# In the first three token pairs one expert's first layer goes by seven products instead of two, and the keys' copies and transposes of later attention groups are queued sooner

## The chip, the core and the metric

The kernel runs on one core of a Trainium2 chip. A core has five engines [...]: TensorE (PE, matrix products; its weight loads are listed as PEld), VectorE (DVE, element-wise work), ScalarE (ACT, exponentials, relu, copies), GpSimd (POOL, here mostly issuing casting loads) and SyncE (SP, issuing loads, stores and transposing transfers). [...] The metric is the device time of one execution in microseconds (us); smaller is better.

## What is computed

Causal attention, where some heads see everything and the others only four sink keys and a window of 64, followed by a mixture of four dense experts, each weighted by a normalised probability per token. Cut to what matters:

```python
# B, H, S, D = 4, 8, 768, 64;  N, DM, E, F = 3072, 512, 4, 1024
scores = q @ k.T / sqrt(D)             # masked: causal, or causal & (sink | window of 64)
a = softmax(scores)                    # per head; 3 heads "retrieval", 5 "streaming"
x = (a @ v).reshape(B * S, H * D)      # 3072 tokens x 512
p = domain_probs / domain_probs.sum(-1)
out = 0
for e in range(4):
    h = maximum(x @ w1[e], 0)          # first layer, 512 -> 1024
    out += p[:, e:e+1] * (h @ w2[e])   # second layer, 1024 -> 512
```

The probabilities are positive, so the kernel scales the inputs of an expert by p before its first layer: relu(p x w1) = p relu(x w1).

## The kernel before

The 3072 tokens are 24 tiles of 128. Attention is done in eight groups of 384 tokens (three tiles; group = batch element b and half c). The experts' work starts while attention is still going on: tiles 0 to 3 go expert by expert in the plain way, and then ten *pairs* of tiles (4 and 5, 6 and 7, ... 22 and 23) follow. Attention for groups 2 to 7 is recorded in small steps between the steps of the pairs; a plan says at which point of the pairs each group is to begin and to end:

```python
UNIT = FTP * DMP * mm_ns(CH) + 3 * FTP * mm_ns(DM)
ONE = E * (FTP * DMP * mm_ns(P) + FTP * mm_ns(DM))
PAIR = 2 * FTP * DMP * mm_ns(PC) + 2 * 7 * HT * KH * mm_ns(P) + 7 * KT * mm_ns(HN)

def att_ns(a):                         # length of a group's attention, for the plan
    ns = 4000.0 if a % NCH == 0 else 6100.0
    ns += NSH * (600.0 if a == 1 else 400.0)
    return ns + (600.0 + HP * 3 * 400.0 if a < NCH else 0.0)
...
begin = E * UNIT + 0.6 * ONE
for a, n in zip(range(2, G), (0.72, 1.65, 3.1, 4.3, 5.95, 7.38)):
    plan[a] = (begin, first_pair + n * PAIR)
    begin = plan[a][1]
```

A pair's first layer gives, per expert, four blocks of relu values in hA. Experts 0 and 1 do it plainly (32 matmuls of 256 columns and four relu evictions on ScalarE). Experts 3 and 2 (EW) do it by Strassen's seven products in Winograd's form (7 x 8 = 56 matmuls of 128 columns), which needs sums of inputs and of results on VectorE:

```python
def plain_layer1(e):                   # yields after each of 4 steps
    xs = scaled(e)
    for f0 in range(0, FTP, 2):
        ps = bank()
        for f in range(2):
            for ct in range(DMP):
                nc.tensor.matmul(out=ps[:, f * PC : (f + 1) * PC],
                    lhsT=w1sb[:, e * DMP + ct, (f0 + f) * P : (f0 + f + 1) * P], rhs=xs[:, ct, :], ...)
        nc.scalar.activation(out=blocks[...], in_=ps..., func=AF.Relu)
        yield 2 * DMP * mm_ns(PC), LSHARE

def scaled_sums(e):                    # three sums of inputs, VectorE
    nc.vector.tensor_tensor(out=x_sum(0), in0=x_part(e, 1, 0), in1=x_part(e, 1, 1), op=ALU.add)
    minus(x_sum(1), x_sum(0), x_part(e, 0, 0))
    minus(x_part(e, 1, 0), x_part(e, 0, 0), x_part(e, 1, 0))

def winograd_layer1(e, x, y):          # yields after each of 7 products of 8 matmuls
    def keep(n, ps): nc.scalar.copy(out=kept[n], in_=ps)
    def add(n, ps, b):                 # block b = relu(product + kept one), VectorE
        nc.vector.tensor_tensor(out=block(b), in0=ps..., in1=kept[n]..., op=ALU.add)
        nc.vector.tensor_scalar(out=block(b), in0=block(b), scalar1=0.0, scalar2=None, op0=ALU.max)
    product(x, w1_part(e, 0, 0), x_part(e, 0, 0), True);  keep(0, x);  yield ns, LSHARE
    z = bank()
    product(z, w1_part(e, 1, 0), x_part(e, 0, 1), True);  add(0, z, 0);  yield ns, LSHARE
    product(x, t(1), x_sum(1), False);  keep(1, x);  yield ns, LSHARE
    product(y, t(0), x_sum(0), True);  keep(2, y)
    minus(x_part(e, 0, 1), x_part(e, 0, 1), x_sum(1));  yield ns, LSHARE
    product(x, w1_part(e, 0, 1), x_part(e, 1, 0), False);  add(2, x, 3);  yield ns, LSHARE
    product(y, w1_part(e, 1, 1), x_part(e, 0, 1), False);  add(1, y, 2);  yield ns, LSHARE
    product(x, t(2), x_part(e, 1, 1), False)
    nc.scalar.activation(out=block(1), in_=x..., func=AF.Relu);  yield ns, LSHARE

a, b = (winograd_layer1(e, *y) for e, y in zip(EW, (banks, banks[::-1])))
n01 = itertools.chain(plain_layer1(0), plain_layer1(1))
early_on = dense(nt0)                  # the first three pairs
for steps, op in (
    ((a, a, n01), lambda: scale_inputs(nt0, EW[1]) if early_on else None),
    ((a, a, n01), lambda: load_probs(nxt) if nxt and not early_on else None),
    ((a, a, n01), lambda: scale_inputs(nt0, 1) if early_on else None),
    ((n01,), lambda: scaled_sums(EW[1])),
    ((a, b, n01), lambda: first_sum(0)),
    ((b, b, n01), lambda: load_probs(nxt) if nxt and early_on else None),
    ((b, b, n01), lambda: last_weight_sum(E - 1) if nt0 == pair0 else None),
    ((b, n01, b), lambda: first_sum(EW[0])),
):
    for x in steps: yield next(x)
    op()
first_sum(1); first_sum(EW[1])
```

The second layer of all four experts together follows, also by seven products, of 16 matmuls of 256 columns each (112 in all), in every pair; this change leaves it alone. Its VectorE work (differences of hA, additions of results, the scaling of the next pair's inputs) is recorded between its products. The sums of expert 2's first-layer weights (t1sb, four VectorE operations of 128x1024) are made while tiles 0 to 3 are worked on.

A group of attention in the later batches runs as follows; kT is one buffer that the transposing transfers of the next group overwrite:

```python
if by_dma:
    keys_to_rows(b, c)                 # kT -> kR, VectorE
    yield 500.0                        # counts as time in the plan
...
for n, h in enumerate(order):          # order = (0, 2, 6, 1, 3, 5, 7, 4)
    ...
    yield from both(scores(h), v_steps)
    ...
    if n == 1 and by_dma:
        keys_to_windows(b, c)          # kT -> kS, VectorE
        sink_rows(b, c)
    if n == 2 and more and g > 1:
        transpose_k(*more)             # the next group's keys -> kT
        load_q(*more)
    ...
if more:
    ...
    transpose_q(*more)
```

Of the kernel before, what the change touches and what calls it, by code (L numbers as in the profile page):

```python
# [18 lines left out]
def kernel(  # L19
# [34 lines left out]
    P = 128  # L54
    B, H, S, D = q.shape
    E, DM, F = moe_w1.shape
    CH = 3 * P
# [222 lines left out]
    def keys_to_windows(b, c):  # L280

        x = windows(kSf)
        for r, n0, hp0, n in ((1, 0, 0, 2), (1, 3, 2, 2), (0, 2, 2, 1)):
            r = half(r)
            src = kT[r, hp0 : hp0 + n, P - WO + NS :]
            step = src.ap[1][0]
            src = bass.AP(
                src.tensor, src.offset, [src.ap[0], [step, n], [WQ, WT], [1, P - NS]]
            )
            dst = x[r, :, n0 : n0 + n, :].rearrange("p t n x -> p n t x")  # L290
            nc.vector.tensor_copy(out=dst[:, :, :, NS:P], in_=src)  # L291
            if c == 0:
                src = kT[r, hp0 : hp0 + n, P : P + NS]
                src = src.rearrange("p n (t x) -> p n t x", t=1)
                nc.vector.tensor_copy(
                    out=dst[:, :, :, 0:NS], in_=src.to_broadcast([D, n, WT, NS])
                )
        if b * NCH + c + 1 < G:
            nc.vector.tensor_copy(out=kT[:, :, P - WO : P], in_=kT[:, :, CH + P - WO :])
# [231 lines left out]
    def mm_ns(cols):  # L531
        return cols / 2.4 + 2.5

    def attention(b, c):
# [282 lines left out]
        if first:  # L817
            yield from transposes(0)
            yield from scores(0)
            sink_row(1)  # L820
            sink_row(3)
            nc.scalar.copy(out=bS[:, 2, :], in_=bS[:, 1, :])
            yield from transposes(1)
            yield from scores(2)
            sink_row(4)
            sink_row(5)
            sink_row(7)
            yield from both(scores(1), values(0))
            yield from transposes(2)
            yield from both(scores(3), values(2))  # L830
            x_transposes(0)
            yield from scores(4)
            yield from transposes(3)
            yield from values(1)
            yield from both(scores(5), values(3))
            yield from both(scores(6), values(4))
            yield from both(scores(7), values(6))
            yield from values(5)
            x_transposes(6)
            yield from values(7)  # L840
            tick(LAG)
            small_things()
        else:
            order = (0, 2, 6, 1, 3, 5, 7, 4) if by_dma else (0, 2, 1, 3, 6, 5, 7, 4)
            more = divmod(g + 1, NCH) if g + 1 < G else None
            if not by_dma:
                sink_rows(b, c)

            def behind_values(h):
                if more and not RETR[h]:  # L850
                    load_v(*more, [h])
            if by_dma:
                keys_to_rows(b, c)
                yield 500.0
            else:
                yield from transposes(0)
                yield from transposes(1)

            waiting = []
            for n, h in enumerate(order):  # L860
                v_steps, done = iter(()), None
                ahead = sum(len(score_tiles(x)) for x in (*waiting, h))
                if len(waiting) > 1 or (waiting and ahead > 6):
                    done = waiting.pop(0)
                    v_steps = values(done)
                yield from both(scores(h), v_steps)
                if done is not None:
                    behind_values(done)
                waiting.append(h)
                if n == 1 and by_dma:  # L870
                    keys_to_windows(b, c)
                    sink_rows(b, c)
                if n == 2 and more and g > 1:
                    transpose_k(*more)

                    load_q(*more)
                if not by_dma and n in (1, 3):
                    yield from transposes({1: 3, 3: 2}[n])
            if more:
                if g == 1:  # L880
                    load_probs(pair0)
                    transpose_k(*more)
                transpose_q(*more)
            for h in waiting:
                yield from values(h)
                behind_values(h)
# [180 lines left out]
    def scale_inputs(nt0, e):  # L1067

        if xs_of[0] is None:
            xs_of[0] = moe.tile([P, E * DMP * PC], FP16, name="xs", tag="xs", bufs=1)  # L1070
        xs = scaled(e)
        for g, c0, t0, n in pieces(nt0):
            require(g)
            xin = xT[g][:, :, c0 : c0 + n * P].rearrange("p c (t x) -> p c t x", t=n)
            o = xs[:, :, t0 * P : (t0 + n) * P].rearrange("p c (t x) -> p c t x", t=n)
            pb = pB_of[nt0][:, t0 : t0 + n, e, :]
            pb = pb.rearrange("p t (c x) -> p c t x", c=1)
            nc.vector.tensor_tensor(  # L1078
                out=o, in0=xin, in1=pb.to_broadcast([P, DMP, n, P]), op=ALU.mult
            )  # L1080
# [25 lines left out]

    def dense(nt0):

        return nt0 < pair0 + 3 * PT

    def pair_steps(nt0, nxt):

# [89 lines left out]

        a, b = (winograd_layer1(e, *y) for e, y in zip(EW, (banks, banks[::-1])))
        n01 = itertools.chain(plain_layer1(0), plain_layer1(1))
        early_on = dense(nt0)
        for steps, op in (
            ((a, a, n01), lambda: scale_inputs(nt0, EW[1]) if early_on else None),  # L1210
            ((a, a, n01), lambda: load_probs(nxt) if nxt and not early_on else None),
            ((a, a, n01), lambda: scale_inputs(nt0, 1) if early_on else None),
            ((n01,), lambda: scaled_sums(EW[1])),
            ((a, b, n01), lambda: first_sum(0)),
            ((b, b, n01), lambda: load_probs(nxt) if nxt and early_on else None),
            ((b, b, n01), lambda: last_weight_sum(E - 1) if nt0 == pair0 else None),
            ((b, n01, b), lambda: first_sum(EW[0])),
        ):
            for x in steps:
                yield next(x)  # L1220
            op()
        first_sum(1)
        first_sum(EW[1])

        o = moe.tile([P, PT, DM], FP32, name="o", bufs=1)
        s = moe.tile([P, 4 * HN], FP32, name="s", tag="sums", bufs=1)
# [80 lines left out]
        add(1, y, 0, 1)  # L1307
        if nxt:
            scale_inputs(nxt, EW[1] if ahead else EW[0])
        store(0)  # L1310
        if last:
            store(1, 1)
# [13 lines left out]
    def moe_steps():  # L1326
        for e in range(E):
            if e == 1:
                turn_probs()
            sums = first_weight_sums(EW[1])[:3] if e == E - 1 else []  # L1330
            steps = plain_steps(0, 3, e, lambda: xT[0], (e % 2) * FTP * CH)
            for n, step in enumerate(steps):
                yield step
                if n > FTP and n % 2 and sums:
                    sums.pop(0)()
            for op in sums:
                op()
            weight_sums(e)
        sums = first_weight_sums(EW[0])
        for e in range(E):  # L1340
            n0 = (e % 2) * FTP * P
            for n, step in enumerate(plain_steps(3, 1, e, lambda: xT[1][:, :, 0:P], n0)):
                yield step
                if n == FTP - 1:
                    sums[e]()
                    if e == EW[1]:
                        first_weight_sums(e)[3]()
            if e + 1 < E:
                last_weight_sum(e)
                (  # L1350
                    lambda: scale_inputs(pairs[0], 0),
                    lambda: scale_inputs(pairs[0], EW[0]),
                    lambda: scaled_sums(EW[0]),
                )[e]()
        for n, nt0 in enumerate(pairs):
            yield from pair_steps(nt0, pairs[n + 1] if n + 1 < len(pairs) else None)
# [19 lines left out]

    UNIT = FTP * DMP * mm_ns(CH) + 3 * FTP * mm_ns(DM)
    ONE = E * (FTP * DMP * mm_ns(P) + FTP * mm_ns(DM))
    PAIR = 2 * FTP * DMP * mm_ns(PC) + 2 * 7 * HT * KH * mm_ns(P) + 7 * KT * mm_ns(HN)

    def att_ns(a):
        ns = 4000.0 if a % NCH == 0 else 6100.0
        ns += NSH * (600.0 if a == 1 else 400.0)
        return ns + (600.0 + HP * 3 * 400.0 if a < NCH else 0.0)

# [1 line left out]

    plan = {1: (1.15 * UNIT, 3.5 * UNIT)}
    begin = E * UNIT + 0.6 * ONE
    for a, n in zip(range(2, G), (0.72, 1.65, 3.1, 4.3, 5.95, 7.38)):  # L1390
        plan[a] = (begin, first_pair + n * PAIR)
        begin = plan[a][1]
    loads(2)
    state = {"a": 1, "steps": None, "done": 0.0}
# [76 lines left out]
```

## Time and profile before

| | before |
|---|---|
| device time, median of 3 | 393.79 us (393.74 to 395.55) |
| span of the profiled execution | 392.0 us |
| granted TensorE clock | 1.0 |
| PE busy | 370.7 us |
| PEld busy | 312.4 us |
| DVE busy | 308.0 us |
| ACT busy | 228.1 us |

Busy times are unions of the recorded intervals of an engine's instructions. Matmuls are pipelined: a recorded matmul of 128 columns lasts 219 ns, but the next starts long before it ends, so PE's busy time says little on how full it is, and the idle time before a matmul understates by the overlap how much later it starts than it could have. A wait of PE in a stretch where PE has more work than any other engine goes straight into the end; a wait of another engine does not.

The pairs are found in the trace by their second layers: the first pair begins at 92.9 us, the second at 126.8, the third at 161.3 and the fourth at 192.4, and the last ends with the kernel.

### The profile page before, as it was taken

To read this page: it belongs to the slowest core of one execution; us is meant where nothing else is said; L and a number is where in the kernel's file an instruction comes from. 1 tells how busy PE (TensorE), PEld (TensorE's weight loads), DVE (VectorE), ACT (ScalarE), POOL (GpSimd) and SP (SyncE) were. 2 spreads that over 40 slices of the span, in tenths; PEclk is the share of its full clock that TensorE was granted. 3 is DMA by queue.
4 is the path that set the end of the run, shared out by engine and by line. 5 is a ranking of instruction groups with operands and counts; after the bars stand their busy time and mean duration, and the time that the engine had idled before them with its cause. 6 is when DMAs were issued, how large, how long until landed. Compare 5 with 4: busy or idle time off the path is not lost.

```text
span 392.0 us, 10589 instructions
## 1 busy us (share of the span) xinstructions
PE 370.7 (95%) x4294; PEld 312.4 (80%) x4294; DVE 308.0 (79%) x714; ACT 228.1 (58%) x476; POOL 111.8 (29%) x152
## 2 busy tenths in 40 slices
PE   8989999989898898799999999899999999999996
PEld 4755456657787797689998888789998999998995
DVE  7736687798887878889978979978958968778671
ACT  3853558636575676566666685476575675361630
POOL 8833652870235034521520236031100000000000
PEclk9999999999999999999999999999999999999999
DMA  8999999998799689988990499394710120200101
GB/s 161 159 208 200 179 183 184 136 186 87 122 76 104 75 122 124 113 122 61 168 73 12 86 191 76 51 181 46 104 52 15 37 86 2 109 2 0 55 3 54
DMA packets 127197, 39.25 MB, mean 100 GB/s; under 512 B 116232, under 2 KB 120876, under 8 KB 127148
## 3 DMA queue, kind: packets, MB, share of 16 engines
q0 software_dynamic: 86816, 19.01, 57.6%
q1 hardware_dynamic: 38732, 19.18, 21.9%
q8 instruction: 33, 0.54, 0.6%
q10 hardware_dynamic: 1600, 0.39, 0.5%
q14 instruction: 16, 0.13, 0.1%
HBM read 44.88 MB, written 6.34 MB: 131 GB/s over the span
## 4 chain that ended last, share of the span: by engine, by line
PE 65%; DVE 16%; DMA 8%; ACT 4%; POOL 3%; issue 3%; SPq 0%; DVEq 0%; POOLq 0%; ACTq 0%
PE pO L1233 26%; PE pA L1119 13%; PE pO L1148 10%; DMA w2sb<-in_moe_w_dram 7%; PE pA L653 4%; DVE xs L1078 3%; PE pO L1017 3%; PE pA L996 3%; DVE hA L1164 2%; PE pA L1148 2%; DVE kS L291 2%; DMA qT<-rows 2%; PE pV L765 2%; PE pV L701 1%; ACT es L671 1%
## 5 line engine op out<-in xcount | busy, mean ns | idle before, releaser
L1233 PEld LDWEIGHTS <-hA 128*128 128x128 f16 x1120 | 105.8, 98 | 12.9 <-issue 0.5
L671 ACT ACTIVATE es<-pA 128x384 f16<-128x384 f32 (+2 forms) x122 | 59.1, 512 | 41.1 <-PE pA L653 36.5
L1119 PE MATMUL pA<-xs,w1sb 128*128 128x256 f16 x640 | 82.0, 273 | 0.9 <-DVE xs L1078 0.9
L1233 PE MATMUL pO<-w2sb,hA 128*128 128x256 f16 x640 | 77.8, 272 | 0.3 <-DVE hA L1164 0.2
L1128 ACT ACTIVATE hA<-pA 128x512 f16<-128x512 f32 x80 | 47.8, 598 | 38.0 <-PE pA L1119 36.4
L1119 PEld LDWEIGHTS <-w1sb 128*128 128x128 f16 x640 | 59.2, 98 | 7.0 <-DVE xs L1078 1.3
L1233 PE MATMUL pO<-tsb,hA 128*128 128x256 f16 x480 | 59.3, 272 | 0.1
L1078 DVE TENSOR_TENSOR xs<-xT,pB 128x1024 f16<-128x1024 f16 (+1 forms) x52 | 49.4, 970 | 0.0
L1148 PEld LDWEIGHTS <-w1sb 128*128 128x128 f16 x640 | 39.6, 98 | 5.4 <-DVE xs L951 3.7
L307 POOL DMA_DIRECT2D vS<-in_v_dram x30 | 29.1, 974 | 46.4 <-PE pV L765 45.1
L951 DVE TENSOR_TENSOR hA<-hA 128x1024 f16<-128x1024 f16 x60 | 39.5, 684 | 0.6 <-PE pO L1233 0.5
L1148 PE MATMUL pO<-xs,w1sb 128*128 128x128 f16 x480 | 35.6, 219 | 3.4 <-DVE xs L951 3.3
L1164 DVE TENSOR_TENSOR hA<-pO,s 128x512 f16<-128x512 f32 x40 | 27.5, 688 | 13.5 <-ACT s L1158 8.0
L1158 ACT COPY s<-pO 128x512 f32<-128x512 f32 x60 | 34.6, 589 | 5.6 <-PE pO L1148 4.0
L212 POOL DMA_DIRECT2D rows<-in_q_dram x15 | 13.3, 895 | 79.4 <-DMA kT<-rows 79.4
L1148 PEld LDWEIGHTS <-t1sb 128*128 128x128 f16 x480 | 30.2, 98 | 3.7 <-DVE kS L951 2.6
L1009 ACT ACTIVATE hA<-pA 128x384 f16<-128x384 f32 (+1 forms) x64 | 22.2, 386 | 18.2 <-PE pA L996 17.7
L996 PE MATMUL pA<-xT,w1sb 128*128 128x384 f16 (+1 forms) x256 | 31.5, 273 | 0.1
L1017 PE MATMUL pO<-w2sb,hA 128*128 128x512 f16 x128 | 30.5, 379 | 0.6 <-DMA w2sb<-in_moe_w_dram 0.6
L788 DVE TENSOR_TENSOR xT<-pV,rc 64x384 f16<-64x384 f32 x37 | 20.5, 555 | 11.1 <-ACT rc L793 8.7
L653 PE MATMUL pA<-qT,kR 128*128 128x384 f16 (+2 forms) x120 | 22.6, 278 | 5.1 <-DVE kR L275 2.4
L783 ACT ACTIVATE rc<-pV,eps 64x384 f32<-64x384 f32 x37 | 21.3, 576 | 7.9 <-PE pV L765 7.2
(134 smaller groups left out, 526.9 us busy)
## 6 DMA issues: line engine op xcount, KB each, us to landing
pB<-p_rows SPq DMA_DIRECT2D x10, 512.0 KB, 6.4
out_dram<-o SPq DMA_DIRECT2D x19, 256.0 KB, 2.2
w1sb<-in_moe_w_dram POOLq DMA_DIRECT2D x8, 512.0 KB, 10.6
w2sb<-in_moe_w_dram POOLq DMA_DIRECT2D x4, 1024.0 KB, 13.4
vS<-in_v_dram POOLq DMA_DIRECT2D x30, 112.0 KB, 4.5
rows<-in_k_dram POOLq DMA_DIRECT2D x18, 128.0 KB, 5.8
rows<-in_q_dram POOLq DMA_DIRECT2D x15, 128.0 KB, 5.6
vR<-in_v_dram POOLq DMA_DIRECT2D x24, 48.0 KB, 5.2
```

Of the source, the lines that this page charges most:

```text
L653: nc.tensor.matmul(out=ps[:, o : o + nq], lhsT=key_tile(b, c, h, t), rhs=qTs[b, c][:, hp, q0 : q0 + nq], start=(n == 0 or not first), stop ...
L671: nc.scalar.activation(out=es[:, 0:cols], in_=ps[:, 0:cols], func=AF.Exp, scale=SC)
L951: nc.vector.tensor_tensor(out=out, in0=a, in1=b, op=ALU.subtract)
L996: nc.tensor.matmul(out=pss[ft][:, 0:cols_n], lhsT=w1sb[:, e * DMP + ct, ft * P : (ft + 1) * P], rhs=x[:, ct, :], start=(n == 0), stop=(n = ...
L1017: nc.tensor.matmul(out=ps_o, lhsT=hs[:, ft, j * P : (j + 1) * P], rhs=w2sb[:, e * FTP + ft, :], start=(ft == 0), stop=(ft == FTP - 1),)
L1078: nc.vector.tensor_tensor(out=o, in0=xin, in1=pb.to_broadcast([P, DMP, n, P]), op=ALU.mult)
L1119: nc.tensor.matmul(out=ps[:, f * PC : (f + 1) * PC], lhsT=w1sb[:, e * DMP + ct, (f0 + f) * P : (f0 + f + 1) * P], rhs=xs[:, ct, :], start= ...
L1128: nc.scalar.activation(out=blocks[:, b0 : b0 + 2, k0 : k0 + 2, :].rearrange("p t f x -> p f t x"), in_=ps.rearrange("p (f t x) -> p f t x" ...
L1148: nc.tensor.matmul(out=ps[:, f * P : (f + 1) * P], lhsT=w[:, ct, f * P : (f + 1) * P], rhs=a[:, ct, :], start=(first and f == 0 and ct == ...
L1158: nc.scalar.copy(out=kept[n], in_=ps)
L1164: nc.vector.tensor_tensor(out=block(b), in0=ps.rearrange("p (f x) -> p f x", f=HT), in1=kept[n].rearrange("p (f x) -> p f x", f=HT), op=AL ...
L1233: nc.tensor.matmul(out=ps, lhsT=a[:, k, :], rhs=b(k), start=(first and k == 0), stop=(k == KT - 1), skip_group_check=not first,)
```

## The change

It has four parts. In the first three pairs (those that `dense` names) only expert 3 goes by seven products; experts 0, 1 and 2 go plainly, in an order of their own that begins with two plain steps and then takes one product of expert 3 after each plain step. The sums of expert 2's weights, which are then needed from the fourth pair on, are moved from the stretch of tiles 0 to 3 into these pairs, one each and the last at the end of the third. Within a later attention group the copies of keys for the windows come after the first head instead of the second, and the next group's transposes of keys and its loading of queries after the second instead of the third. The plan gives the copies of keys more time (1500 instead of 500) before the first head's scores, sets the groups' ends a little differently, and lets groups from the third on begin 0.08 of a pair after the last one's end. It is meant to take work from VectorE where attention and pairs run together, and to give what TensorE waits for more time to be ready. The diff, cut to its core:

```diff
             if by_dma:
                 keys_to_rows(b, c)
-                yield 500.0
+                yield 1500.0
...
+                if n == 0 and by_dma:
+                    keys_to_windows(b, c)
                 if n == 1 and by_dma:
-                    keys_to_windows(b, c)
                     sink_rows(b, c)
-                if n == 2 and more and g > 1:
+                if n == 1 and more and g > 1:
                     transpose_k(*more)
                     load_q(*more)
...
+    more_weight_sums = iter(first_weight_sums(EW[1]))
...
+        if dense(nt0):
+            n = itertools.chain(*(plain_layer1(e) for e in range(E - 1)))
+            order = (
+                ((n,), lambda: scale_inputs(nt0, 1)),
+                ((n,), None),
+                ((n, a), lambda: last_weight_sum(E - 1) if nt0 == pair0 else None),
+                ((n, a), lambda: scale_inputs(nt0, 2)),
+                ((n, a), lambda: load_probs(nxt)),
+                ((n, a), lambda: first_sum(0)),
+                ((n, a), next(more_weight_sums)),
+                ((n, a), None),
+                ((n, a), lambda: first_sum(1)),
+                ((n,), lambda: first_sum(EW[0])),
+                ((n, n), lambda: first_sum(2)),
+            )
+        else:
+            n = itertools.chain(plain_layer1(0), plain_layer1(1))
+            order = (                      # as before, but first_sum(EW[0]) one group sooner
+                ((a, a, n), None),
+                ((a, a, n), lambda: load_probs(nxt) if nxt else None),
+                ((a, a, n, n), lambda: scaled_sums(EW[1])),
+                ((a, b, n), lambda: first_sum(0)),
+                ((b, b, n), None),
+                ((b, b, n), lambda: first_sum(EW[0])),
+                ((b, n, b), lambda: (first_sum(1), first_sum(EW[1]))),
+            )
...
+        if ahead and dense(nt0):           # end of the third pair
+            next(more_weight_sums)()
...
-            sums = first_weight_sums(EW[1])[:3] if e == E - 1 else []
...                                         # and the fourth sum, for tiles 0 to 3
-    PAIR = 2 * FTP * DMP * mm_ns(PC) + 2 * 7 * HT * KH * mm_ns(P) + 7 * KT * mm_ns(HN)
+    PAIR = LSHARE * (2 * FTP * DMP * mm_ns(PC) + 2 * 7 * HT * KH * mm_ns(P))
+    PAIR += PSHARE * 7 * KT * mm_ns(HN)
     def att_ns(a):
         ns = 4000.0 if a % NCH == 0 else 6100.0
+        ns += 1000.0 if a >= NCH else 0.0
...
-    for a, n in zip(range(2, G), (0.72, 1.65, 3.1, 4.3, 5.95, 7.38)):
-        plan[a] = (begin, first_pair + n * PAIR)
+    for a, n in zip(range(2, G), (0.74, 1.7, 3.1, 4.3, 5.95, 7.35)):
+        plan[a] = (begin + (0.08 * PAIR if a > 2 else 0.0), first_pair + n * PAIR)
```

More of the change, by code (lines that the diff above doesn't have):

```diff
@@ L1206, in pair_steps @@
         a, b = (winograd_layer1(e, *y) for e, y in zip(EW, (banks, banks[::-1])))
[L1207 to L1218, printed above, removed]
+        if dense(nt0):
[24 more added lines that the diff above has]
+            )
+        for steps, op in order:
             for x in steps:
                 yield next(x)
-            op()
-        first_sum(1)
-        first_sum(EW[1])
+            if op is not None:
+                op()
         o = moe.tile([P, PT, DM], FP32, name="o", bufs=1)
@@ L1329, in moe_steps @@
                 turn_probs()
-            sums = first_weight_sums(EW[1])[:3] if e == E - 1 else []
[L1331 to L1337, printed above, removed]
+            yield from plain_steps(0, 3, e, lambda: xT[0], (e % 2) * FTP * CH)
             weight_sums(e)
@@ L1345, in moe_steps @@
                     sums[e]()
-                    if e == EW[1]:
-                        first_weight_sums(e)[3]()
             if e + 1 < E:
```

## The prediction, made before the changed kernel was run

> **What bounds the kernel now.** I read the busy times and slices first, then the chain, then PE's waits, and last the lines of PE and VectorE around single waits. The page's first part and the table of stretches, here cut at the starts of the pairs (columns: length, busy us and count of each engine, clock, share of DMA, GB/s):
>
> ```profile
> PE 370.7 (95%) x4294; PEld 312.4 (80%) x4294; DVE 308.0 (79%) x714; ACT 228.1 (58%) x476; POOL 111.8 (29%) x152
> ```
>
> ```profile
> 92.90:126.76 33.86, 30.34 (x405) 27.23 (x402) 28.58 (x72) 21.73 (x43) 11.66 (x14) 1.00 0.83 95
> 126.76:161.26 34.50, 30.89 (x412) 27.71 (x411) 28.17 (x70) 23.12 (x46) 11.40 (x14) 1.00 1.08 103
> 161.26:192.40 31.14, 29.18 (x395) 26.68 (x392) 28.83 (x69) 19.30 (x38) 9.22 (x11) 1.00 1.06 105
> ...
> 337.60:363.30 25.70, 25.70 (x294) 23.70 (x293) 19.02 (x39) 10.34 (x20) 0.00 (x0) 1.00 0.12 46
> ```
>
> The reader is to see that a pair with no attention beside it takes 25.7 us with PE never idle, while the first three take 31 to 34.5 us with 2 to 3.6 us of idle PE each, although VectorE, at 28 to 29 us, is below the length too. PE is the bound, held up in places by VectorE. In the chain that ended last PE has 65% and DVE 16%; its DVE pieces between 74 and 167 us are exactly the sums and input scalings of the pairs. PE's waits between 80 and 170 us (total, times, longest):
>
> ```profile
> PE pO L1148 <- DVE xs L951: 3.3, 3, 1.6
> PE pA L653 <- DVE kR L275: 2.4, 2, 1.2
> PE pA L653 <- DMA qT<-rows: 2.0, 1, 2.0
> PE pO L1148 <- DVE kS L951: 1.3, 1, 1.3
> PE pA L1119 <- DVE xs L1078: 0.9, 2, 0.5
> PE pO L1233 <- DVE hA L1164: 0.2, 1, 0.2
> ```
>
> That is 10.1 us in 10 waits. A 128-column matmul is recorded as 219 ns, but 16 of them in a row advance by 0.89 us, 56 ns each; so each wait costs some 0.16 us more than its idle time. Adding that up, start against start, and with two smaller delays (of 0.18 and 0.31 us) that leave no idle time, I get 12.2 us in this stretch: 88.1 us 1.34 and 0.18 (kR, exp), 98.9 1.72, 103.1 0.70, 110.1 0.35, 122.2 1.40 (kR), 132.6 1.22, 136.6 0.54, 151.7 0.31, 157.6 2.20 (queries' transposes), 164.5 1.46, 167.8 0.83. Elsewhere after 60 us I find only some 4 us, most between 205 and 256. One of these waits, on PE and on VectorE:
>
> ```profile
> 96.72 0.61 PE L1148 MATMUL pO<-xs,w1sb 128*128 128x128 f16 x8
> 98.89 0.62 PE L1148 MATMUL pO<-xs,w1sb 128*128 128x128 f16 x8 [1.56 <-DVE xs L951]
> ```
>
> ```profile
> 96.35 0.68 DVE L1164 TENSOR_TENSOR hA<-pA,s 128x512 f16<-128x512 f32 x1
> ...
> 97.41 1.22 DVE L1078 TENSOR_TENSOR xs<-xT,pB 128x1024 f16<-128x1024 f16 x1
> 98.54 0.28 DVE L951 TENSOR_TENSOR xs<-xs,kS 128x256 f16<-128x256 f16 x1
> ```
>
> The sixth product of expert 3 needs the difference of 0.28 us, and the fifth product, 0.45 us, is all that lies between its request and its use. It stands behind a scaling of 1.22 us.
>
> [...] the trace has 684 ns for 1024 fp16 elements and 688 ns for only 512 from PSUM. So taking results from PSUM by VectorE additions, as the seven products do, is its dear part. [...]
>
> **The change part by part.**
>
> *Expert 2 goes plainly in three pairs: PE pays.* 56 matmuls at 56 ns are 3.12 us; 32 at 109 ns are 3.50. So +0.38 us a pair, +1.15 us in all, on the path. ScalarE stays level: three keeps and a relu of about 0.59 us against four relus of 0.598.
>
> *VectorE is relieved.* Per pair it loses the three input sums (3 x 0.284), three additions (3 x 0.688), three relus (3 x 0.325) and the difference (0.29): 4.2 us. It gets one weight sum of 0.69. Net 3.5 us of 28 in the first two pairs, where it came closest to the bound; the third gets two weight sums, net 2.8. None of this is directly in the time. Some 2.8 us of weight sums leave the stretch from 74 to 92 us, where they stood ahead of the key copies for which PE waited 1.34 us.
>
> *The order gives slack.* The changed program's order shows, before expert 3's first product, two or three plain steps (0.87 us each), and between its fifth and sixth product, as between any two, one more. From the request to the use of the difference there are now two plain steps and a product, 2.2 us and what attention adds, instead of 0.45. The inputs of expert 1 are needed after four plain steps and attention scores, some 4.5 us into the pair; ahead of them VectorE has about 3 to 4 us of work. Those of expert 2 are needed after eight plain steps and five products, over 9 us. So the waits at 98.9, 103.1, 132.6, 136.6, 164.5 and 167.8 (6.5 us) should mostly go, and that at 110.1 (0.35), for the last block of additions is now asked for three plain steps before the second layer.
>
> *Attention starts later in the pair.* Group 2's first scores, which stood ahead of the last expert of tile 3, now stand after it, about 3.5 us later; those of group 3 come after the last 24 of the pair's matmuls that they preceded (2.6 us); those of group 4 some 6 us later, past the landing of the queries' transposes, which took 6.3 us from 151.2 us on. That covers the waits of 1.34, 0.18, 1.40 and 2.20 us: 5.1 us.
>
> Sum: 12.2 us of waits, less 1.15 for matmuls. I don't give all of the waits back. In the first layer of pair 1 I add up VectorE's operations in the changed order and get about 16.3 us against PE's 15.3 with attention, since the late start pushes work of tile 3 and of the window copies (2.4 us) into it; the second layer is level at about 13.8. Residual waits of 0.5 to 1.5 us a pair are likely, 3 us in all. Later, groups 5 and 7 stand bunched in the second layer of one pair, which costs VectorE in the next pair's first layer; against it the sooner window copies should spare the wait of about 1 us at 248. I put that at zero. 393.8 - 12.2 + 3.0 + 1.15 = 385.8.
>
> **The rivals.** First, VectorE becomes the bound in these pairs: the same attention must fit between a later start and nearly unchanged ends, so freed VectorE time is filled again, and PE waits for other blocks. For it speak the 16.3 against 15.3 us; against it that VectorE is relieved by 2.8 to 3.5 us and what PE needs is asked for early. It would keep 6 to 7 us of waits: about 389.5. Second, the waits were slack: PE delayed in the pairs delays nothing that later slack doesn't hide. Against it speaks that from 260 us on PE has no idle time of note, so whatever is saved arrives at the end. It would give 393 to 395. Third, the bunched groups make new waits of 2 to 4 us in pairs 5 and 8; before, the similar bunch in pair 4 was followed by 0.5 us of waits in pair 5's first layer and some 2 more by 256 us. That is 388 to 390. Fourth, all waits go, with those after 205 us halved: 381.
>
> **Range and chances.** The certain term is +1.15; the uncertain one is how much of 12.2 comes back: 4 us of it puts the time at 391, 12.2 and a little more at 382.5. The limit of 2% is at 385.9, almost on my sum, so the chance of faster by over 2% is about a half; slower by 2% would need 9 us of new waits.
>
> **What would show it.** Right: PE's waits on L951, kR and qT between 85 and 195 us down from 12 to about 3 us; the first three pairs at about 31, 31 and 29 us; 168 fewer matmuls of 128 columns in the first layer and 96 more of 256 (3 x 56 and 3 x 32); VectorE busy about 12 us less. Wrong: waits of plain steps on L1078, of the second layer on sums of hA, or of scores and values on ScalarE's exponentials in pairs 4, 5, 7 and 8, that add to more than 5 us.

## The result and the profile after

The changed kernel takes 389.43 us (median of 4, 388.57 to 389.74) against 393.76 us before: 1.2% less, ratio 0.9876 with a 95% interval of 0.9844 to 0.9907. The prediction was 385.8 us with a range of 382.5 to about 391: the time is inside, but only about half of the predicted gain arrived.

The page's busy times, and the same cut by pairs as before (each pair from the end of the last one's second layer to the end of its own; columns: length, busy us and count of each engine, clock, share of DMA, GB/s):

```profile
PE 372.5 (96%) x4222; PEld 313.9 (81%) x4222; DVE 296.1 (76%) x684; ACT 228.1 (59%) x476; POOL 109.6 (28%) x152
```

```profile
91.18:120.13 28.95, 28.95 (x361) 26.41 (x359) 25.31 (x61) 20.34 (x40) 7.52 (x8) 1.00 0.94 98
120.13:152.81 32.68, 31.79 (x402) 28.48 (x400) 25.50 (x61) 23.85 (x47) 12.34 (x14) 1.00 0.99 107
152.81:182.78 29.97, 29.49 (x364) 26.56 (x362) 25.71 (x64) 20.37 (x41) 11.83 (x14) 1.00 1.00 106
...
215.58:245.63 30.05, 28.20 (x348) 25.52 (x345) 23.54 (x57) 18.34 (x36) 12.39 (x14) 1.00 1.18 106
```

VectorE's busy time fell by 12 us, as forecast, and the first pair now runs without a gap on PE. But in the fifth pair, the last line, PE is idle for 1.85 us (30.05 less 28.20). PE's waits from 80 us to the end of the third pair:

```profile
PE pV L765 <- DVE xT L788: 0.9, 2, 0.6
PE pV L701 <- ACT es L671: 0.3, 1, 0.3
PE pO L1152 <- DVE hA L1168: 0.2, 1, 0.2
```

Those of pairs 4 to 8, first in the kernel before (191.4 to 338 us), then in the changed one (182.8 to 334 us):

```profile
PE pA L653 <- DVE kS L295: 0.8, 1, 0.8
PE pO L1148 <- DVE kS L951: 0.6, 1, 0.6
PE pV L701 <- DVE es L675: 0.2, 1, 0.2
PE pO L1148 <- ACT s L1158: 0.2, 1, 0.2
```

```profile
PE pO L1152 <- ACT s L1162: 1.4, 4, 0.5
PE pO L1250 <- DVE hA L1168: 1.4, 3, 0.9
PE pV L765 <- issue: 1.0, 1, 1.0
PE pO L1152 <- ACT hA L1132: 0.6, 1, 0.6
PE pO L1152 <- DVE o L1271: 0.5, 2, 0.3
...
```

In the first stretch 10.1 us of idle have become 1.4. In pairs 4 to 8, in which the change leaves the experts' matmuls as they were, 1.8 us have become 5.8, in waits mostly of other kinds. The account, as in the prediction start against start (what a matmul starts later than the one before it lets it; short delays that the list of waits leaves out are in it). The kernel before is cut in the same way, so that its second, third and fourth pair begin at 126.3, 161.1 and 191.4 us; the starts given ahead of the prediction are late by 0.2 to 1.0 us.

| stretch | length before | after | waits before | after |
|---|---|---|---|---|
| up to the first pair | 92.9 | 91.2 | 13.8 (rough) | 12.9 (rough) |
| pairs 1 to 3 | 98.5 | 91.6 | 11.05 | 2.3 |
| pairs 4 to 8 | 146.3 | 150.7 | 4.6 | 9.1 |
| pairs 9 and 10, to the last matmul | 51.1 | 51.1 | 0.0 | 0.0 |
| behind the last matmul | 3.2 | 3.2 | | |
| sum | 392.0 | 387.8 | | |

At the start of the fourth pair the changed kernel is 8.6 us ahead, with the same attention done (some 22.6 us of PE work both times), and then it loses 4.4. In what follows I compare the stretches from the first pair on. Each kernel has one trace, but where programs agree their traces do: in pairs 1 to 3 to 0.1 us, and in pairs 4 to 8 the changed kernel, e5 and e11 below last 150.7 to 150.9 us. The first stretch does not repeat so: in kernels with the same program it lasts 89.7 to 91.7 us. In the longest two, this one and e4, the mean granted clock of the trace is 0.996 and 0.995; in this one it was 0.51 in the 3.4 us from 20.9 us on and 1.00 beside them. The changed kernel's three runs with such a mean clock (0.995 to 0.996) took 389.3 to 389.7 us against 388.6 for the one with 1.0.

The wait shown before the change, for the difference that the sixth product needs, in the new order. PE from expert 3's fourth product to its fifth, and VectorE:

```profile
98.42 0.61 PE L1152 MATMUL pO<-kS,t1sb 128*128 128x128 f16 x8
98.86 0.35 PE L701 MATMUL pV<-vR,es 128*128 128x65 f16 x6
99.05 1.03 PE L1123 MATMUL pA<-xs,w1sb 128*128 128x256 f16 x8
99.92 0.61 PE L1152 MATMUL pO<-xs,w1sb 128*128 128x128 f16 x8
```

```profile
98.15 1.22 DVE L1079 TENSOR_TENSOR xs<-xT,pB 128x1024 f16<-128x1024 f16 x1
99.28 0.28 DVE L675 TENSOR_TENSOR es<-es,mC 128x256 f16<-128x256 f16 x1
99.48 0.28 DVE L952 TENSOR_TENSOR xs<-xs,kS 128x256 f16<-128x256 f16 x1
```

It still stands behind a scaling of 1.22 us, but is done at 99.76 us, before even the fifth product starts.

### The profile page after: what moved, and what is told of

Same layout as the page of the kernel before. It is cut to its first block, busy times and chain, and to the rows that moved or that the text cites. A ratio compares the mean times of both kernels' runs of the same rounds, so it can differ in the third digit from the quotient of the medians.

```text
span 387.8 us, 10400 instructions
## 1 busy us (share of the span) xinstructions
PE 372.5 (96%) x4222; PEld 313.9 (81%) x4222; DVE 296.1 (76%) x684; ACT 228.1 (59%) x476; POOL 109.6 (28%) x152
## 4 chain that ended last, share of the span: by engine, by line
PE 72%; DVE 14%; ACT 5%; issue 3%; POOL 3%; DMA 2%; POOLq 0%; ACTq 0%; DVEq 0%
PE pO L1250 23%; PE pA L1123 17%; PE pO L1152 10%; PE pA L997 7%; PE pO L1018 7%; PE pA L653 4%; DVE xs L1079 3%; DVE hA L952 3%; DMA vS<-in_v_dram 2%; PE pV L701 2%; DVE xT L788 2%; PE pA L1152 1%; DVE hA L1168 1%; PE pV L765 1%; ACT s L1162 1%
## 5 line engine op out<-in xcount | busy, mean ns | idle before, releaser
L1123 PE MATMUL pA<-xs,w1sb 128*128 128x256 f16 x736 | 93.3, 273 | 0.0
L1132 ACT ACTIVATE hA<-pA 128x512 f16<-128x512 f32 x92 | 55.0, 598 | 33.5 <-PE pA L1123 33.2
L1123 PEld LDWEIGHTS <-w1sb 128*128 128x128 f16 x736 | 68.8, 98 | 7.0
L1152 PEld LDWEIGHTS <-w1sb 128*128 128x128 f16 x544 | 33.9, 98 | 2.3 <-issue 1.4
L1168 DVE TENSOR_TENSOR hA<-pO,s 128x512 f16<-128x512 f32 x34 | 23.3, 686 | 14.5 <-ACT s L1162 8.3
L1162 ACT COPY s<-pO 128x512 f32<-128x512 f32 x51 | 29.4, 587 | 5.2 <-PE pO L1152 4.0
L1152 PE MATMUL pO<-xs,w1sb 128*128 128x128 f16 x408 | 29.9, 219 | 1.0 <-ACT s L1162 0.5
L1152 PEld LDWEIGHTS <-t1sb 128*128 128x128 f16 x408 | 25.9, 98 | 4.2 <-issue 1.7
L1268 ACT COPY s<-pO 128x256 f32<-128x256 f32 x30 | 11.2, 372 | 26.8 <-PE pO L1250 22.3
```

The source lines that it names most:

```text
L1123: nc.tensor.matmul(out=ps[:, f * PC : (f + 1) * PC], lhsT=w1sb[:, e * DMP + ct, (f0 + f) * P : (f0 + f + 1) * P], rhs=xs[:, ct, :], start= ...
L1132: nc.scalar.activation(out=blocks[:, b0 : b0 + 2, k0 : k0 + 2, :].rearrange("p t f x -> p f t x"), in_=ps.rearrange("p (f t x) -> p f t x" ...
L1152: nc.tensor.matmul(out=ps[:, f * P : (f + 1) * P], lhsT=w[:, ct, f * P : (f + 1) * P], rhs=a[:, ct, :], start=(first and f == 0 and ct == ...
```

## The experiments

**First: which part makes the new waits?** Theory A: the new plan bunches groups 5 to 7. Theory B: the pairs' part makes them. Theory C: the sooner copies and transposes do. Four kernels, timed beside the kernel before, whose median was 394.19 us here.

e1, the first part alone:

```diff
 # the kernel before, with
+        if dense(nt0): n = itertools.chain(*(plain_layer1(e) for e in range(E - 1))); order = (...)
+        else: order = (... ((b, b, n), lambda: first_sum(EW[0])), ...)   # as in the change
+        if ahead and dense(nt0): next(more_weight_sums)()
 # keys, transposes and plan untouched
```

> The kernel before with the first part of the change alone (three pairs with expert 3 alone by seven products, in the new order, and the weight sums moved into them); the attention's plan and the places of copies and transposes stay as before. Theory A (the plan and its gaps bunch groups 5 to 7 and so make the new waits from the fourth pair on; the pairs' part makes none): PE's waits from the fourth pair on stay at the 4.6 us of before, the six waits on sums and scalings of the first three pairs go, some of the three waits on kR and qT stay; 387 to 389 us. Theory B (the new waits come from the pairs' part, for instance its weight sums and its later start): waits from the fourth pair on near 9 us and 391 us or more.

e2, the attention's parts alone:

```diff
-                yield 500.0
+                yield 1500.0
+                if n == 0 and by_dma: keys_to_windows(b, c)
+                if n == 1 and more and g > 1: transpose_k(*more); load_q(*more)
+    for a, n in zip(range(2, G), (0.74, 1.7, 3.1, 4.3, 5.95, 7.35)):   # and the rest of the plan
 # pairs untouched
```

> The kernel before with the attention's parts alone: copies and transposes sooner, 1500 before the first scores, the new plan; the pairs as before. Theory A: the waits on kR and qT (5 us) go, the six on sums and scalings (6.5 us) stay or grow, and the waits from the fourth pair on rise from 4.6 to 8 or 9 us: 392 to 395 us. Theory B: the waits from the fourth pair on stay at 4.6 us: 388 to 390 us.

e3, the changed kernel with the late groups' plan as before:

```diff
-                yield 1500.0
+                yield 1500.0 if g < 5 else 500.0
-        ns += 1000.0 if a >= NCH else 0.0
+        ns += 1000.0 if NCH <= a < 5 else 0.0
-    ... (0.74, 1.7, 3.1, 4.3, 5.95, 7.35) ... 0.08 * PAIR if a > 2 else 0.0
+    ... (0.74, 1.7, 3.1, 4.3, 5.95, 7.38) ... 0.08 * PAIR if 2 < a < 5 else 0.0
```

> The changed kernel with the plan of groups 5 to 7 as before (no gap, 500 before the first scores, end 7.38); copies and transposes stay sooner. Theory A: the waits from the fourth pair on fall from 9.1 to about 5 us and the time to 385 to 386. Theory C (it is the sooner copies and transposes that make them): they stay near 9 us and the time at 389.

e4, the changed kernel with the late groups' copies and transposes where they were:

```diff
-                if n == 0 and by_dma:
+                if n == (0 if g < 5 else 1) and by_dma:
-                if n == 1 and more and g > 1:
+                if n == (1 if g < 5 else 2) and more and g > 1:
```

> The changed kernel with the copies for the windows and the next group's transposes of groups 5 to 7 where they were (after the second and third head). Theory A: no change worth the name, 388.5 to 390 us, waits from the fourth pair on 8 to 10 us. Theory C: they fall to about 5 us and the time to 385 to 386.

| | median us | ratio (95%) | waits, pairs 1-3 | waits, pairs 4-8 |
|---|---|---|---|---|
| before | 394.19 | | 11.05 | 4.6 |
| e1 | 390.01 | 0.9873 (0.9828 to 0.9919) | 4.2 | 6.9 |
| e2 | 389.74 | 0.9876 (0.9830 to 0.9922) | 6.7 | 6.5 |
| after | 389.43 | 0.9876 (0.9844 to 0.9907) | 2.3 | 9.1 |
| e3 | 387.53 | 0.9822 (0.9765 to 0.9878) | 2.3 | 7.5 |
| e4 | 388.65 | 0.9841 (0.9796 to 0.9885) | 2.3 | 8.3 |

Each part alone gives about what both give together. In the first three pairs they take different waits: e1 those on sums, and it leaves those at the starts of groups (kR 1.4 us, queries' transposes 2.1 us); e2 takes the latter. But each brings about 2 us of new waits to pairs 4 to 8 (2.3 and 1.9), together about the 4.4 of the change, though not all at the same places. So A, which gave everything to the plan, is refuted as it stands, and so is B. e3 misses Theory A's 5 us: only 1.6 of 4.4 come back. e4 misses C's: 0.8.

e1 points to the pairs' part, which in the order of pairs 4 to 8 changes one line: the sum of expert 3's blocks (L1101) now stands ahead of expert 2's sixth product and the addition that takes its result, instead of behind the seventh. In the changed kernel, PE around the start of the fifth pair's second layer, and VectorE:

```profile
230.58 0.61 PE L1152 MATMUL pO<-xs,t1sb 128*128 128x128 f16 x8
232.06 1.03 PE L1250 MATMUL pO<-w2sb,hA 128*128 128x256 f16 x8 [0.86 <-DVE hA L1168]
```

```profile
230.28 0.56 DVE L788 TENSOR_TENSOR xT<-pV,rc 64x384 f16<-64x384 f32 x1
230.86 0.43 DVE L1101 TENSOR_TENSOR hA<-hA 128x512 f16<-128x512 f16 x1
231.31 0.69 DVE L1168 TENSOR_TENSOR hA<-pO,s 128x512 f16<-128x512 f32 x1
```

The second layer's first product is written to the bank (pO has two) that held expert 2's sixth product, and that is read last by the addition at 231.31. That addition ends at 232.00 us, and PE starts at 232.06. The sum ahead of it, 0.43 us, is first used by a sum that VectorE makes after that first product. Such waits stand at the start of the second layer in pairs 4, 5, 6 and 8: 0.21, 1.03, 0.34 and 0.52 us, 2.1 together; the kernel before has one, of 0.28 us in pair 4, and e2, which kept the sum's place, none in these pairs.

**Second: that line, the cause in the first pairs, and more pairs in the new order.** (Kernel before: 393.88 us.)

e5 puts VectorE work back into the first three pairs, for which nothing waits:

```diff
+        def extra(n):                     # after three of the steps; 6 + 6 additions a pair
+            for _ in range(4 if n == 1 else 1):
+                nc.vector.tensor_tensor(out=spare, in0=t[:, 0:256], in1=t[:, 256:512], op=ALU.add)
+            for _ in range(2):
+                nc.vector.tensor_tensor(out=spare, in0=t32[:, 0:256], in1=t32[:, 256:512], op=ALU.add)
```

> The changed kernel with VectorE work put back into each of the first three pairs that nothing waits for: six additions of 128x256 fp16 and six of 128x256 fp32 (about 6 x 0.28 + 6 x 0.42 = 4.2 us, what expert 2's sums cost) into a spare tile, beside expert 3's products. Theory D (what counts there is the slack of the new order): waits of the first three pairs rise from 2.3 by less than 1.5 us, and the time by as little. Theory E (what counts is that VectorE is relieved): they rise by 4 us or more and the time to 392 or above.

e6:

```diff
-                ((b, b, n), lambda: first_sum(EW[0])),
-                ((b, n, b), lambda: (first_sum(1), first_sum(EW[1]))),
+                ((b, b, n), None),
+                ((b, n, b), lambda: (first_sum(EW[0]), first_sum(1), first_sum(EW[1]))),
```

> The changed kernel with one line of the other seven pairs as before: the sum of expert 3's blocks (first_sum(EW[0])) is recorded after expert 2's last product, not just ahead of its last addition. Theory F (standing ahead of that addition it holds back the bank that the second layer's first product writes): the waits at the starts of second layers (2.1 us in pairs 4, 5, 6 and 8) go, the waits from the fourth pair on fall from 9.1 to about 7 us, the time to about 387.5. Theory A (all of the new waits come from the plan): they stay near 9 us.

e7, on top of e6, and e8 with e3's plan besides:

```diff
-        return nt0 < pair0 + 3 * PT
+        return nt0 < pair0 + 8 * PT
```

> As e6_sum_at_end, and the first eight pairs, not three, in the new order with expert 3 alone by seven products (the fourth weight sum then stands at the end of the eighth). PE pays 5 x 0.38 = 1.9 us more. Theory D: the waits in the first layers of pairs 4 to 8 (6.3 us in the changed kernel, of which some 2 go with the sum) nearly vanish; 384.5 to 386.5 us. If the bunched attention holds PE in the second layers as much, the waits only move there: 387 to 389 us.

> As e7_eight_dense_pairs, with the plan of groups 5 to 7 as in e3_late_plan_before (spread over more of the pairs, no gap, 500 before the first scores). Theory A: 1 to 2 us below e7_eight_dense_pairs, 383.5 to 385.5 us. If slack in the first layers makes the plan indifferent: within 0.7 us of it; the waits on kR at 232 us (1.0) would stay either way.

| | median us | ratio (95%) | waits, pairs 1-3 | waits, pairs 4-8 |
|---|---|---|---|---|
| e5 | 392.50 | 0.9962 (0.9947 to 0.9978) | 6.1 | 9.3 |
| e6 | 386.44 | 0.9794 (0.9742 to 0.9845) | 2.3 | 7.0 |
| e7 | 382.62 | 0.9691 (0.9648 to 0.9734) | 1.8 | 1.1 |
| e8 | 381.31 | 0.9661 (0.9619 to 0.9704) | 1.8 | 0.6 |

e5: the added operations took 288 and 425 ns each, 4.3 us a pair, and brought 3.8 us of waits back in three pairs. That is close to Theory E, which asked for 4 us or more. The 425 ns are those with fp32 operands in SBUF; the second layer's additions from PSUM, of the same 128x256, took 421 in the changed kernel, so that PSUM alone makes an addition dear, as the prediction took it, is not shown. The chief new ones (e5's line numbers are one to thirteen higher):

```profile
PE pO L1153 <- DVE hA L1169: 1.6, 1, 1.6
PE pO L1153 <- DVE xs L953: 0.7, 2, 0.4
```

e6: as Theory F has it, the waits from the fourth pair on fall by 2.1 us. Of the 2.1 at the starts of second layers 1.5 go; one of 0.6 is left, in pair 5, with the addition now directly behind the attention's scaling:

```profile
230.06 1.03 PE L1250 MATMUL pO<-w2sb,hA 128*128 128x256 f16 x8 [0.42 <-DVE hA L1168]
```

The other 0.6 goes at attention's steps in pair 4 and at the start of pair 6. (Of the 3.1 us between the traces of e6 and the changed kernel, 1.0 lies ahead of the pairs, where their programs agree.)

e7 and e8: with expert 2 plain in every pair that has attention beside it, PE pays 1.9 us more for matmuls and, against e6, saves 6 us of waits; e8 is 12.6 us faster than the kernel before, and 8.1 us faster than the change. Its pairs 4 and 5 (compare 30.05 us with 28.20 busy above for the fifth):

```profile
181.44:212.17 30.73, 30.73 (x375) 27.71 (x372) 22.91 (x54) 20.87 (x41) 6.32 (x8) 1.00 0.82 89
212.17:241.00 28.83, 28.80 (x343) 25.91 (x341) 22.24 (x58) 18.78 (x37) 11.48 (x14) 1.00 1.24 121
```

The plan alone (e7 to e8) moves 0.5 us of waits. The two medians differ by 1.3, but the traces, 379.9 and 379.7 us long, by 0.2; the rest is not explained.

**Third: does the account close?** (Kernel before: 393.37 us.)

e9 is e6 with e3's plan; e10 is e9 with e4's places; e12 is e6 with the gap alone taken away (0.08 * PAIR if 2 < a < 5). e11 is the changed kernel with the old interleaving in the first three pairs:

```diff
-                ((n,), lambda: scale_inputs(nt0, 1)), ((n,), None), ((n, a), ...), ((n, a), ...), ...
+                ((a, a, n), lambda: scale_inputs(nt0, 1)), ((a, a, n), None),
+                ((a, a, n), lambda: scale_inputs(nt0, 2)), ((n,), lambda: load_probs(nxt)),
+                ((a, n), lambda: first_sum(0)), ((n, n), ...), ((n,), ...), ((n,), ...), ((n,), ...), ((n, n), ...)
```

> The changed kernel with both undone that are suspected of the new waits: the sum of expert 3's blocks at the end of the first layer (as in e6_sum_at_end) and the plan of groups 5 to 7 as before (as in e3_late_plan_before); three pairs in the new order. If the two causes add up (sum 2.1, plan 1.5 us in the single runs): waits from the fourth pair on 5 to 5.8 us and 384.5 to 386 us. If the plan's effect was a mere exchange of waits: 6.5 to 7 us, as with the sum alone.

> As e9_sum_end_late_plan, and the window copies and transposes of groups 5 to 7 where they were before: from the fourth pair on nothing of the change is left but the start of groups. If the account is complete, waits from the fourth pair on are back at the 4.6 us of before, within 0.7; and the time is 384.5 to 386 us. If they stay above 6 us, some cause is not named yet (the gap of groups 3 and 4, the weight sums at the end of the third pair).

> The changed kernel with the first three pairs' steps interleaved as before: two products of expert 3 for each plain step from the start, so that the fifth product alone lies between the request and the use of the difference for the sixth, and four plain steps in a row at the end; expert 2 stays plain and VectorE relieved. Theory D (slack of the order counts): waits of the first three pairs rise from 2.3 to 5 us or more. Theory E (VectorE's relief counts): they rise by less than 1.5 us.

> As e6_sum_at_end, without the gap of 0.08 of a pair ahead of groups 5 to 7 (the 1500 before the first scores stays). If the gap is what bunches the groups: waits from the fourth pair on fall from 7.0 to 5 or 5.5 us, as with the whole of the late plan. If it is the 1500: they stay between 6.5 and 7.5 us.

| | median us | ratio (95%) | waits, pairs 1-3 | waits, pairs 4-8 |
|---|---|---|---|---|
| e9 | 386.66 | 0.9830 (0.9793 to 0.9868) | 2.3 | 6.85 |
| e10 | 386.34 | 0.9825 (0.9789 to 0.9861) | 2.3 | 6.9 |
| e11 | 389.16 | 0.9888 (0.9860 to 0.9917) | 3.1 | 9.1 |
| e12 | 385.70 | 0.9801 (0.9771 to 0.9832) | 2.3 | 6.2 |

e9 is the surprise: with the sum in its old place the old plan saves 0.1 us, within what the traces repeat to. It exchanges waits. In pairs 4, 5 and 8 it takes away 3.8 us (the groups are no longer bunched there), and in the second layer of pair 5 and at the start of that of pair 7 it adds 3.4. Read the other way, from e3 to e9, the sum's old place saves 0.65 us with the old plan, where it saved 2.1 with the new one: the two effects don't add. PE's waits of e9 in pairs 4 to 8:

```profile
PE pO L1152 <- DVE kS L952: 1.5, 2, 1.0
PE pO L1250 <- DVE hA L1168: 1.0, 1, 1.0
PE pO L1250 <- DVE hA L952: 0.9, 1, 0.9
PE pA L653 <- DVE kR L275: 0.7, 1, 0.7
PE pO L1152 <- ACT s L1162: 0.5, 1, 0.5
```

e10 refutes Theory C with the others undone too, and says that the account is not complete: 6.9 us, not 4.6. e12 recovers 0.8 of the 7.0, less than the gap would have to if it were the cause. What is left, 2.3 us, I can't tie to one edit, but e1 narrows it. e1 has none of the attention's edits, and yet PE's attention work of pairs 4 to 8 stands in it layer by layer where it stands in e10: 0.44 us of it in pair 4's first layer, against 0.22 before. That is because the steps of the first pairs, now longer, count in the plan. And pairs 5 and 6 wait 4.4 us in e1 and 4.7 in e10, against 3.0 before, two of e1's waits being these, the first of 0.6 us and the second absent in the kernel before:

```profile
PE pO L1150 <- DVE kS L951: 1.0, 1, 1.0
PE pA L653 <- DVE kR L275: 0.7, 1, 0.7
```

So more than half of the 2.3 comes with the pairs' part, without any edit of attention and, as e10 has the sum in its old place, without the sum. That the shift of attention by a step makes it is likely, but it was not tried alone. Besides, e10's fourth pair has a wait of 0.6 us in its first layer (e1: 0.3, before: none), on a sum of inputs that stands behind the fourth weight sum; that was not tried alone either.

e11: the old interleaving costs 0.8 us of waits once VectorE is relieved: Theory E. As in the kernel before, it is not the fifth product alone that lies between the request and the use of the difference, but a plain step and the fifth product.

## Why the prediction was right and wrong

- **PE pays 1.15 us**: right. 168 matmuls of 128 columns went and 96 of 256 came; each counted at the usual distance of its shape in the trace before (0.89 us for 16 of 128 columns, 0.87 for eight of 256), the whole trace's rose by 1.06 us.
- **The waits of the first three pairs**: 12.2 us, from the 88.1 us one on, to about 3. They came to 2.3. The size was right; the reason given for half of it was not. "The order gives slack" was to take away 6.5 us. e11 takes the slack of expert 3's products away, on which 5.2 of the 6.5 us stood (the early scaling of expert 1's inputs stays), and 0.8 us come back; e5 takes VectorE's relief away, keeps the slack, and 3.8 come back (for the places where e5 puts its work). The slack was also misread. In the kernel before, too, a plain step stands between expert 3's fourth product, with which the difference is requested, and the sixth:

```profile
94.77 1.06 PE L1148 MATMUL pO<-kS,t1sb 128*128 128x128 f16 x16
95.67 1.04 PE L1119 MATMUL pA<-xs,w1sb 128*128 128x256 f16 x8
```

  The fourth product ends the first line, at 95.66 us, and the sixth could have begun at 97.17 without its wait of 1.72. So 1.5 us lay there and not 0.45, and the change added one plain step of 0.87. What the prediction called "none of this is directly in the time" is the larger share. Its working looked at the one operation that stood ahead of a needed sum; how long VectorE's whole queue was behind was not in it, though the 16.3 us against 15.3 in its residual term were just that. The first rival, VectorE as the bound, named the right engine, but the 6 to 7 us of waits that it would keep did not stay.
- **Attention starts later**: right for 3.6 of its 5.1 us: e1 keeps the waits on kR and the queries' transposes in these pairs (3.5 us), e2 and the change don't. The 1.34 us at 88.1, ahead of the pairs, shrink to 0.26 in e1 as well, which leaves attention alone but takes the weight sums out of that stretch; either part is enough for it.
- **Residual waits of 0.5 to 1.5 us a pair**: 0.1, 1.3 and 0.9.
- **"I put that at zero"**, of pairs 4 to 8: the step that failed. It measured +4.4 us, more than the whole of the 3.6 us by which 385.8 was missed; with the 4.4 the prediction would have been 390.2, and the stretches up to the third pair did a little better than it said. The wait at 248 us was spared, as forecast; the new ones outweigh it. The third rival, bunched groups, named 388 to 390 us, and that is where the time fell, in part by luck: its new waits were to stand in pairs 5 and 8, which got 1.2 of the 4.4, while pairs 4 and 6 got 3.3. And up to 2.1 of the 4.4 (e6; 0.65 with the old plan, e9) were another thing that the prediction had read past: a 0.43 us sum recorded sooner. The diff has the line, remarked as one group sooner; the prediction doesn't speak of it. With that sum and, for groups 5 to 7, the plan and the places of copies and transposes as before, 2.3 us stay (e10), whose cause is open.
- The second rival (slack hides what is saved) is refuted: pairs 9 and 10 take 51.1 us in every trace, so what reaches them arrives at the end, as the prediction said.

## What to carry to other kernels

At 230.86 us above VectorE took its operations in the order in which they are recorded: the sum that was put forward took 0.43 us, and the addition behind it started at 231.31, 0.45 us after the sum had. Before moving an operation forward, look for what stands behind it that somebody waits for soonest, a bank that must come free included. Where a bound engine waits on a second one in many places, count the second one's work per stretch first; slack in the order brought 0.8 us here where VectorE's relief brought 3.8, and 0.38 us more for PE in a pair was cheap against 3.5 us off VectorE. And if it pays in the stretches that were looked at, try it in all with the same company: the change stopped at three pairs of eight.

## What was not expected of the hardware

The trace repeats far more closely than the times do. From the first pair on, 91.6 us of three pairs with some 1,100 matmuls agreed within 0.02 us in the traces of seven kernels with the same program there, while the stretch ahead of them varied by 2 us, and the medians of one kernel's times by as much as 0.8 us from one set of runs to the next (the kernel before: 393.37, 393.88 and 394.19). For a change of 1% the stretches of a profile told more than the medians.
